# Instruction queues ordered by latest possible time instead of by age, in a planned long-convolution and FFN training step

## The chip, the cores and the metric

The kernel runs on one core of a Trainium2 chip. The metric is the device time in microseconds of one execution. Beside it stands one profiled execution, whose span is the time from its first to its last instruction.

## The reference

The kernel computes the output of a gated block and the gradients of all its inputs, for a sequence of 2048 rows of 512 channels in bf16. Cut to what matters:

```python
xn = layernorm(A_u)                                    # 2048 x 512
dt = exp(log_dt)                                       # per channel
P  = exp(dt * (A_re + 1j * A_im) * l)                  # 512 channels x 128 states x 2048 steps
K  = real(einsum("dn,dnl,dn->dl", C, P, dt * B))       # a long convolution kernel per channel
s  = irfft(rfft(xn) * rfft(K))[:2048] + xn * Dskip     # long convolution over the sequence
h  = silu(xn @ w1)                                     # 512 -> 1792
g  = silu(h @ w2)                                      # 1792 -> 512
out = A_u + s * g
# and the vector-Jacobian product with grad_out: gradients of A_u, A, B, C (re, im), log_dt, Dskip, w1, w2
```

## The kernel before

**Work and stages.** The channels are four blocks of 128. In order of the program: a setup (layer norm of the rows, constants, magnitudes of the state powers); the tables (`gen_tables`: sines on ACT, products on DVE, and on PE the convolution kernels' values), the forward convolutions by a discrete Fourier transform on PE (`gen_conv_x`, `gen_conv_fwd`), and beside them the FFN forward (`gen_ffn_fwd`, 8 chunks of 256 rows, L812 and L829); a gate stage (`gen_gate_rows`) that makes `ds` with Silu (L864) and `do` with its derivative (L873); the convolution backward (`gen_conv_bwd`) beside the FFN's backward for the activations (`gen_ffn_da`, L1173 and L1184, which loads `dhT` at L1149 and stores it at L1178); the state-space backward (`gen_ssm_bwd`, 16 groups of products, L961 to L1037) beside the rest of that; then the weight gradients (`gen_dw2` L1216, `gen_dw1` L1234) and the layer norm's backward (`gen_ln_bwd`, L1266 to L1279). Spectra, activations and tables that don't fit in SBUF go through DRAM. All evacuations of PSUM are in one helper, L295 on ACT and L296 on DVE.

**What sets the order.** The stages are Python generators, and `interleave`, `woven` and `paced` draw from them with fixed weights; that gives one order of all instructions, the program order. At its end `Plan` takes that list and makes a queue for each engine. It works out the dependencies (`deps`: reads, writes, buffers that are used again), and pairs that only say that one instruction may not start before another has started (`starts`: the first users of one tag's tiles in order, and pools that share memory). `cost` gives each instruction a time on its engine and a time to completion. `solve` then plays the program forwards in time: an instruction is ready when all it depends on is done, and when an engine is free it takes a ready instruction. Among those ready it takes the one with the smallest number, which is the oldest in program order: its age decides. DMAs are sent by the queue of the engine that issues them (SP for most), in the plan's order, and share one modelled line: 900 ns, the time of the packets, then 1200 ns to completion. A function on ACT whose table isn't loaded costs 1283 ns more. PE runs at half rate when a window of 3413 ns was too idle. `apply` fixes the result, by an order edge from each instruction to the next on its engine:

```python
        edge = mybir.DependencyInfo(mybir.DependencyClass.NoSync, mybir.DependencyReason.DATA)
        for line in self.plan.values():
            for a, b in zip(line, line[1:]):
                self.tc.add_manual_dep(self.ins[b], self.ins[a].name, edge, reason="plan")
```

On the chip each engine goes through its queue in that order, and waits where what it needs isn't there yet.

**The opening of the state-space backward.** `gen_ssm_bwd` first loads all six parameter matrices transposed (`load_params`, L609), then folds the gradients of block 0 (`ssm_fold`: four loads of `GE` at L961, then products on PE from L977), and loads the turned tables `YT` (L999) and `Eb` (L992) of the first group. All these go through SP's queue.

Of the kernel before, what the change touches and what calls it, by code (L numbers as in the profile page):

```python
# [34 lines left out]
class Plan:  # L35
# [5 lines left out]
    def __init__(self, nc, tc):  # L41
        self.tc, self.ins, self.deps, self.starts = tc, [], [], []
        cells, users, first, tags, pools, before, old, placed = {}, {}, {}, {}, {}, {}, {}, []
        held = {"left": [], "right": []}
        bounds = {p.alloc_inst.name: (p, True) for p in tc.info.pools}
        bounds.update({p.release_inst.name: (p, False) for p in tc.info.pools if p.release_inst is not None})
        for x in nc.cur_bb.bb.instructions:
            if x.name in bounds:
                p, opens = bounds[x.name]
                if str(p.space) == "SB":  # L50
                    h = held[str(p.side)]
                    if opens:
                        lo = h[-1][1] if h else 0
                        hi = lo + sum(m.bufs * m.max_size_bytes for m in p.tag_meta.values()) // P
                        h.append((p.id, hi))
                        placed.append((p.id, lo, hi) if str(p.side) == "left" else (p.id, self.ROOM - hi, self.ROOM - lo))
                    else:
                        h[:] = [y for y in h if y[0] != p.id]
                continue
            ap_of = lambda args: [a.bass_ap for a in args if getattr(a, "bass_ap", None) is not None]  # L60
            outs, ins = ap_of(x.outs), ap_of(x.ins)
            if not outs:
                continue
            n, eng, dep = len(self.ins), x.engine.name, set()
            if type(x).__name__ == "InstMatmult" and not x.start_tensor_calc:
                ins = ins + outs
            self.ins.append(x)
            spots = []
            for ap, writes in [(a, False) for a in ins] + [(a, True) for a in outs]:
                t = ap.tensor  # L70
                tag = getattr(t, "tag", None)
                if tag is None:
                    if not writes:
                        continue
                elif t.name not in users:
                    same = tags.setdefault(tag, [])
                    bufs = t.tag_meta.bufs
                    before[t.name] = first[same[-1]] if same and str(t.space) != "DRAM" else None
                    if len(same) >= bufs and str(t.space) != "DRAM":
                        old[t.name] = users[same[-bufs]]  # L80
                    same.append(t.name)
                    first[t.name], users[t.name] = n, set()
                if tag is not None:
                    dep |= old.get(t.name, set())
                    if before[t.name] is not None and before[t.name] != n:
                        self.starts.append((before[t.name], n))
                    users[t.name].add(n)
                    pools.setdefault(int(tag.rsplit("_", 1)[1]), set()).add(n)
                q, idx, size = self.cells(ap)
                last, readers = cells.setdefault(t.name, (np.full(size, -1, np.int32), {}))  # L90
                spots.append((writes, q, idx, last, readers))
                for k in q:
                    for r in [last] + (list(readers.values()) if writes else []):
                        dep.update(np.unique(r[k, idx]).tolist())
            for writes, q, idx, last, readers in spots:
                for k in q:
                    if writes:
                        last[k, idx] = n
                        for r in readers.values():
                            r[k, idx] = -1  # L100
                    else:
                        readers.setdefault(eng, np.full(last.shape, -1, np.int32))[k, idx] = n
            self.deps.append(dep - {-1, n})
        for i, (a, a0, a1) in enumerate(placed):
            for b, b0, b1 in placed[i + 1:]:
                if a0 < b1 and b0 < a1 and a in pools and b in pools:
                    self.starts.append((pools[a], pools[b]))

    @staticmethod
    def cells(ap):  # L110
# [71 lines left out]
                break  # L182
        return r

    def solve(self):

        N = len(self.ins)
        succ, wait = [[] for _ in range(N)], [len(d) for d in self.deps]
# [4 lines left out]
        groups = []  # L193
        for a, b in self.starts:
# [3 lines left out]
            else:  # L198
# [2 lines left out]
                    begun[m].append(-len(groups))  # L201
                for m in b:
                    wait[m] += 1
        cost = [self.cost(x) for x in self.ins]
        eng = [x.engine.name for x in self.ins]
        dma = ["DMA" in type(x).__name__ or "Dma" in type(x).__name__ for x in self.ins]
        ready = {e: [] for e in set(eng)}
        free = dict.fromkeys(ready, 0.0)
        line, tables = 0.0, "nesd"
        heat, warm = {}, {0: False}  # L210
        self.plan = {e: [] for e in ready}
        events, self.start = [], [0.0] * N
        for n in range(N):
            if not wait[n]:
                events.append((0.0, 1, n))
# [2 lines left out]
        end = 0.0  # L218

        def met(m, t):  # L220
            wait[m] -= 1
            when[m] = max(when[m], t)
            if not wait[m]:
                heapq.heappush(events, (when[m], 1, m))

        def clock(t):
            w = int(t // 3413)
            for v in range(max(warm), w):
                warm[v + 1] = heat.get(v, 0.0) / 3413 > (0.35 if warm[v] else 0.5)
            return warm[w]  # L230
        while events:
            t, kind, n = heapq.heappop(events)
            if kind == 1:
                heapq.heappush(ready[eng[n]], n)
                e = eng[n]
            else:
                e = n
            while ready[e] and free[e] <= t:
                n = heapq.heappop(ready[e])
                d, l = cost[n]  # L240
                if e == "PE":
                    if not clock(t):
                        l += max(d, 25.0)
                        d *= 2
                    heat[int(t // 3413)] = heat.get(int(t // 3413), 0.0) + d
                elif e == "Activation" and not dma[n]:
                    f = self.SETS.get(getattr(self.ins[n], "func", None))
                    if f:
                        both = "".join(c for c in f if c in tables)
                        if not both:  # L250
                            d, l = d + 1283.0, l + 1283.0
                        tables = both or f[0]
                self.plan[e].append(n)
                self.start[n] = t
                free[e] = t + d
                heapq.heappush(events, (free[e], 2, e))
                if dma[n]:
                    line = max(line, t + (d if e == "Pool" else min(d, 330.0)) + 900.0) + l
                    done = line + 1200.0
                else:  # L260
                    done = t + l + self.SEM
                end = max(end, done)
                for m in succ[n]:
                    met(m, t + d if e == "PE" == eng[m] else done)
                for m in begun[n]:
                    if m >= 0:
                        met(m, t)
                    else:
                        g = groups[-m - 1]
                        g[0] -= 1  # L270
                        if not g[0]:
                            for y in g[1]:
                                met(y, t)
        assert sum(map(len, self.plan.values())) == N, "the plan is not complete"
        return end

    def apply(self):
# [1015 lines left out]
def kernel(ctx, tc, A_u, A_A_re, A_A_im, A_B_re, A_B_im, A_C_re, A_C_im, A_log_dt, A_Dskip, B_x, B_w1, B_w2, grad_out,  # L1293
# [140 lines left out]
    es_b.close()  # L1434
    interleave([gen_ln_bwd(k, pool("lw", side="right")), dw], [1, 1])
    plan = Plan(nc, tc)
    plan.solve()
    plan.apply()
# [1 line left out]
_INS = ['A_u', 'A_A_re', 'A_A_im', 'A_B_re', 'A_B_im', 'A_C_re', 'A_C_im', 'A_log_dt', 'A_Dskip', 'B_x', 'B_w1', 'B_w2', 'grad_out']  # L1440
# [26 lines left out]
```

## Time and profile before

| | us |
|---|---|
| median of 3 runs | 701.69 |
| lowest, highest | 695.24, 705.36 |
| the profiled execution | 696.09 |
| its span | 694.4 |
| PE, DVE, ACT busy | 573.5, 521.0, 470.8 |
| mean granted TensorE clock | 0.950 |

The profile's page names groups of instructions by line, engine, and output and input tiles. PE is TensorE's matmuls, PEld its weight loads, DVE VectorE, ACT ScalarE, POOL GpSimd, SP SyncE; a name such as SPq is the engine's sequencer, which issues DMAs. A digit in a row of slices is the busy share of a fortieth of the span in tenths; PEclk is the clock that PE was granted, in tenths. In a timeline a row has its start, its duration, the engine, the line, the operation, the tiles and a count, and in brackets how long the engine was idle before it and what released it.

### The profile page before, as it was taken

Reading aid. Unit: us, or ns where it says so; the run is one execution under the profiler, and the core shown is the slowest. Engines: PE = TensorE matmul, PEld = TensorE weight load, DVE = VectorE, ACT = ScalarE, POOL = GpSimd, SP = SyncE. Lnnn points to the kernel's source line nnn. Section 1 sums busy time; section 2 is a strip of 40 time slices with the busy share of each in tenths; the row PEclk is TensorE's granted clock in tenths of the full one; section 3 lists DMA queues with packets and bytes.
Section 4 is the critical chain, followed back from the end, with each engine's and each line's share of the span. In section 5 each row is a group of like instructions: output and inputs, shape, how many; then the busy total and the mean of one; then the engine's idle time right before and its main releaser. Section 6 shows DMA issues by size and latency. Waiting matters only on the chain.

```text
span 694.4 us, 15206 instructions
## 1 busy us (share of the span) xinstructions
PE 573.5 (83%) x6268; PEld 416.6 (60%) x6268; DVE 521.0 (75%) x917; ACT 470.8 (68%) x630; POOL 79.9 (12%) x163
## 2 busy tenths in 40 slices
PE   0599697878979785469998998928998879999988
PEld 0455564547657564256765756626966656865877
DVE  6959987979989585869797979415798533966971
ACT  6959765978887988997867775406648438744541
POOL 1274100010001000000000000000002020023211
PEclk9989998999999998779999999978999999999999
DMA  9864536584557487968886775594899996747994
GB/s 297 331 145 154 196 142 225 206 274 168 189 192 260 178 292 259 287 227 274 263 273 204 236 228 176 144 236 116 168 215 221 223 252 147 172 124 243 261 253 124
DMA packets 158773, 148.85 MB, mean 214 GB/s; under 512 B 79280, under 2 KB 136112, under 8 KB 155120
## 3 DMA queue, kind: packets, MB, share of 16 engines
q1 hardware_dynamic: 145664, 125.07, 63.0%
q0 software_dynamic: 6144, 17.83, 7.1%
q10 hardware_dynamic: 6896, 4.98, 2.3%
q8 instruction: 49, 0.80, 0.5%
q14 instruction: 20, 0.16, 0.1%
HBM read 65.14 MB, written 64.36 MB: 187 GB/s over the span
## 4 chain that ended last, share of the span: by engine, by line
PE 48%; ACT 20%; DVE 13%; DMA 9%; issue 4%; SPq 4%; ACTq 2%; DVEq 0%
PE ps_w L1234 6%; PE ps_o L829 6%; PE ps_dx L1184 5%; PE ps_w L1216 5%; PE ps_da L1173 4%; ACT dA L295 4%; PE ps_h L812 2%; ACT mag_all L635 2%; PE psS L1032 2%; PE ps_i L573 2%; ACT sn L684 2%; PE pt_t L362 2%; PE ps_v L1010 2%; PE ps_i L582 2%; PE psS L1036 2%
## 5 line engine op out<-in xcount | busy, mean ns | idle before, releaser
L295 ACT CAST dA<-ps_s 128x1024 bf16<-128x1024 f32 x96 | 94.0, 1032 | 14.5 <-PE ps_s L541 9.9
L829 PE MATMUL ps_o<-W,aT 128*128 128x512 bf16 x224 | 62.8, 417 | 11.9 <-ACT hT L295 11.6
L812 PE MATMUL ps_h<-XT,W 128*128 128x256 bf16 x448 | 60.3, 279 | 6.5 <-DVE XT L296 5.0
L1173 PE MATMUL ps_da<-doT,W 128*128 128x256 bf16 x448 | 60.9, 276 | 3.1 <-ACT doT L295 1.8
L1020 DVE TENSOR_TENSOR Tp<-Vb,Eb 128x1344 bf16<-128x1344 bf16 x64 | 52.6, 855 | 10.2 <-ACT Vb L295 7.8
L1175 DVE TENSOR_TENSOR dhT<-ps_da,dhT 128x512 bf16<-128x512 f32 x56 | 37.7, 686 | 28.7 <-PE ps_da L1173 28.5
L295 ACT CAST dB<-ps_i 128x1024 bf16<-128x1024 f32 x48 | 47.0, 1027 | 17.3 <-PE ps_i L573 14.2
L295 ACT CAST Vb<-ps_v 128x672 bf16<-128x672 f32 x64 | 44.0, 740 | 18.8 <-PE ps_v L1010 15.2
L1184 PE MATMUL ps_dx<-W,dhT 128*128 128x512 bf16 x224 | 55.5, 380 | 0.0
L1216 PE MATMUL ps_w<-YD,a_tok 128*128 128x512 bf16 x224 | 53.4, 379 | 0.5 <-ACT a_tok L1201 0.5
L812 PEld LDWEIGHTS <-W 128*128 128x128 bf16 x448 | 42.4, 100 | 18.4 <-issue 10.9
L295 ACT CAST o<-ps_w 128x256 bf16<-128x256 f32 (+1 forms) x42 | 18.7, 445 | 50.0 <-PE ps_w L1234 28.1
L1234 PE MATMUL ps_w<-dh_tok,xn 128*128 128x256 bf16 x448 | 49.4, 273 | 3.1 <-DMA dh_tok<-DHd 3.1
L1173 PEld LDWEIGHTS <-W 128*128 128x128 bf16 x448 | 41.3, 99 | 13.4 <-issue 6.2
L1234 PEld LDWEIGHTS <-xn 128*128 128x128 bf16 x448 | 43.7, 98 | 8.9 <-DMA dh_tok<-DHd 2.1
L829 PEld LDWEIGHTS <-aT 128*128 128x128 bf16 x224 | 21.2, 105 | 37.9 <-issue 17.9
L573 PE MATMUL ps_i<-I,sp_in 64*128 64x128 bf16 x768 | 32.5, 229 | 11.6 <-DVE sp_in L596 8.7
L573 PEld LDWEIGHTS <-sp_in 64*128 64x128 bf16 x768 | 23.8, 99 | 24.5 <-DVE sp_in L596 12.3
L295 ACT CAST hT<-ps_h 128x512 bf16<-128x512 f32 x56 | 32.1, 617 | 8.1 <-PE ps_h L812 4.9
L296 DVE COPY dB<-pt_f 128x2048 bf16<-128x2048 bf16 x24 | 28.3, 1218 | 11.4 <-PE pt_f L547 11.4
L557 PE MATMUL ps_s<-dB,F 128*64 128x512 bf16 x192 | 29.5, 389 | 7.1 <-ACT dA L295 5.3
L295 ACT CAST pd_s<-ps_dx 128x512 bf16<-128x512 f32 x16 | 9.4, 590 | 35.7 <-DMA Pd<-pd_s 17.0
(222 smaller groups left out, 1301.9 us busy)
## 6 DMA issues: line engine op xcount, KB each, us to landing
Yd<-YD SPq DMA_DIRECT2D x8, 1024.0 KB, 5.3
sp_in<-Ud SPq DMA_DIRECT2D x8, 1024.0 KB, 8.1
h_in<-Hd SPq DMA_DIRECT2D x14, 512.0 KB, 4.8
Ed<-E SPq DMA_DIRECT2D x8, 672.0 KB, 4.0
Eb<-Ed SPq DMA_DIRECT2D x8, 672.0 KB, 5.6
Hd<-hT POOLq DMA_DIRECT2D x8, 512.0 KB, 5.8
Ud<-dA SPq DMA_DIRECT2D x4, 1024.0 KB, 4.8
KXd<-dA SPq DMA_DIRECT2D x4, 1024.0 KB, 6.0
```

What stands on the lines that cost most here:

```text
L295: return self.nc.scalar.copy(out=out, in_=in_)
L296: return self.nc.vector.tensor_copy(out=out, in_=in_)
L557: nc.tensor.matmul(out=ps[64 * h:64 * h + 64, 4 * v:4 * v + 4], lhsT=k.F2[:, c, :], rhs=Bv[:, u, v, h], start=True, stop=True)
L573: nc.tensor.matmul(out=ps[:, h, g], lhsT=Y[hs, c, 4 * q + g, :], rhs=k.I2[hs, c].rearrange("p c m -> p (c m)"), start=(c == 0), stop=(c == 1))
L812: nc.tensor.matmul(out=ps[:, j], lhsT=k.W1[:, dk, ft * P:ft * P + P], rhs=XTv[:, :, dk, :], start=(dk == 0), stop=(dk == DK - 1))
L829: nc.tensor.matmul(out=ps[:], lhsT=aT[:, ft, t * P:t * P + P], rhs=k.W2[:, ft, :], start=(ft == 0), stop=(ft == FT - 1))
L1020: k.nc.vector.tensor_tensor(out=Tp[:, c, :, r ^ c].rearrange("p e (q w) a -> p q w e a", w=2), in0=Vb[:, :, c].rearrange("p q w (e a) -> p ...
L1173: nc.tensor.matmul(out=ps[:, j], lhsT=k.W2[:, ft, dk * P:dk * P + P], rhs=dTv[:, :, dk, :], start=(dk == 0), stop=(dk == DK - 1))
L1175: nc.vector.tensor_tensor(out=dh[:, i0:i0 + 2, :], in0=ps[:], in1=dh[:, i0:i0 + 2, :], op=ALU.mult)
L1184: nc.tensor.matmul(out=ps[:], lhsT=dhs[ft // 8][:, ft % 8, t * P:t * P + P], rhs=k.W1[:, :, ft * P:ft * P + P], start=(ft == 0), stop=(ft ...
L1216: nc.tensor.matmul(out=ps[:], lhsT=at[:, t, :], rhs=k.do[:, t, :], start=(t == 0), stop=(t == k.T - 1))
L1234: nc.tensor.matmul(out=ps[:], lhsT=k.xn[:, t, dk * P:dk * P + P], rhs=dh[:, t].rearrange("p j n -> p (j n)"), start=(t == 0), stop=(t == k ...
```

## The change

`solve` takes a list `age` by which the ready instructions are ranked. A new function `back` plays the same program from its end backwards, with the same costs: an instruction is ready when all that depend on it are placed, and among those ready on an engine the one that the forward plan completed last goes first. It returns for each instruction how long before the end it must start at the latest. `search` runs `solve` once by age, then six times `back` and `solve` in turn, where the instruction with the longest time to the end goes first; the plan with the shortest modelled end of these six is kept (the plan by age isn't one of them). New pairs in `starts` make the last user of each tile, in program order, start after all its other users. No instruction of the device is added or taken away. `back` knows no function tables and no slow PE clock; `solve` still does. The diff, cut:

```diff
             self.deps.append(dep - {-1, n})
+        self.starts += [(m, max(u)) for u in users.values() for m in u if m != max(u)]
...
-    def solve(self):
+    def solve(self, age):
...
             if kind == 1:
-                heapq.heappush(ready[eng[n]], n)
+                heapq.heappush(ready[eng[n]], (age[n], n))
                 e = eng[n]
             else:
                 e = n
             while ready[e] and free[e] <= t:
-                n = heapq.heappop(ready[e])
+                n = heapq.heappop(ready[e])[1]
...
-                end = max(end, done)
+                end, self.done[n] = max(end, done), done
...
+    def back(self):
+
+        N, cost, eng, dma = len(self.ins), self.costs, self.eng, self.dma
+        left, before, groups = [0] * N, [[] for _ in range(N)], []
+        for d in self.deps:
+            for m in d:
+                left[m] += 1
...
+        need, late = [0.0] * N, [0.0] * N
+        ready = {e: [] for e in set(eng)}
+        free = dict.fromkeys(ready, 0.0)
+        line, queue, events = 0.0, [], []
+
+        def met(m, t):
+            left[m] -= 1
+            need[m] = max(need[m], t)
+            if not left[m]:
+                heapq.heappush(events, (need[m], 2, m) if dma[m] else (max(0.0, need[m] - cost[m][0]), 1, m))
+        for n in range(N):
+            if not left[n]:
+                left[n] = 1
+                met(n, 1200.0 if dma[n] else cost[n][1])
+        while events:
+            t, kind, n = heapq.heappop(events)
+            if kind == 2:
+                heapq.heappush(queue, (-self.done[n], n))
+            if kind > 1 and kind < 4:
+                while queue and line <= t:
+                    n = heapq.heappop(queue)[1]
+                    line = t + cost[n][1]
+                    heapq.heappush(events, (line, 3, n))
+                    d = cost[n][0]
+                    heapq.heappush(events, (line + 900.0 - (0.0 if eng[n] == "Pool" else max(0.0, d - 330.0)), 1, n))
+                continue
+            if kind == 1:
+                heapq.heappush(ready[eng[n]], (-self.done[n], n))
+                e = eng[n]
+            else:
+                e = n
+            while ready[e] and free[e] <= t:
+                n = heapq.heappop(ready[e])[1]
+                free[e] = late[n] = t + cost[n][0]
+                heapq.heappush(events, (free[e], 4, e))
+                for m in self.deps[n]:
+                    met(m, late[n] + (1200.0 if dma[m] else cost[m][0] if e == "PE" == eng[m] else cost[m][1] + self.SEM))
...
+        return late
+
+    def search(self, rounds):
+
+        self.solve(range(len(self.ins)))
+        best = None
+        for _ in range(rounds):
+            end = self.solve([-t for t in self.back()])
+            if best is None or end < best[0]:
+                best = end, self.plan, self.start
+        end, self.plan, self.start = best
+        return end
...
-    plan.solve()
+    plan.search(6)
     plan.apply()
```

More of the change, by code (lines that the diff above doesn't have):

```diff
@@ L107, in __init__ @@
                     self.starts.append((pools[a], pools[b]))
+        self.costs = [self.cost(x) for x in self.ins]
+        self.eng = [x.engine.name for x in self.ins]
+        self.dma = ["DMA" in type(x).__name__ or "Dma" in type(x).__name__ for x in self.ins]
     @staticmethod
@@ L203, in solve @@
                     wait[m] += 1
-        cost = [self.cost(x) for x in self.ins]
-        eng = [x.engine.name for x in self.ins]
-        dma = ["DMA" in type(x).__name__ or "Dma" in type(x).__name__ for x in self.ins]
+        cost, eng, dma = self.costs, self.eng, self.dma
         ready = {e: [] for e in set(eng)}
@@ L211, in solve @@
         self.plan = {e: [] for e in ready}
-        events, self.start = [], [0.0] * N
+        events, self.start, self.done = [], [0.0] * N, [0.0] * N
         for n in range(N):
@@ L274, in solve @@
         assert sum(map(len, self.plan.values())) == N, "the plan is not complete"
+        return end
[5 more added lines that the diff above has]
+                left[m] += 1
+        for a, b in self.starts:
+            if isinstance(a, int):
+                before[b].append(a)
+                left[a] += 1
+            else:
+                groups.append([len(b), a])
+                for m in b:
+                    before[m].append(-len(groups))
+                for m in a:
+                    left[m] += 1
+        need, late = [0.0] * N, [0.0] * N
[26 more added lines that the diff above has]
+                e = eng[n]
+            else:
+                e = n
[5 more added lines that the diff above has]
+                    met(m, late[n] + (1200.0 if dma[m] else cost[m][0] if e == "PE" == eng[m] else cost[m][1] + self.SEM))
+                for m in before[n]:
+                    if m >= 0:
+                        met(m, late[n])
+                    else:
+                        g = groups[-m - 1]
+                        g[0] -= 1
+                        if not g[0]:
+                            for y in g[1]:
+                                met(y, late[n])
+        return late
```

## The prediction

> **What bounds the kernel now.** I first read the top of the page: busy times, then the slices.
>
> ```profile
> span 694.4 us, 15206 instructions
> PE 573.5 (83%) x6268; PEld 416.6 (60%) x6268; DVE 521.0 (75%) x917; ACT 470.8 (68%) x630; POOL 79.9 (12%) x163
> PE   0599697878979785469998998928998879999988
> PEclk9989998999999998779999999978999999999999
> ```
>
> No engine is full. PE has the most work, 573.5 of 694.4 us, so 121 us of it are gaps, and the slices show where: the first two, four around slice 15, one hole at slice 26 (a 2), and a tenth to a third of every slice between 4 and 14. I cut the span there, into five stages, and asked for the busy times of each.
>
> ```profile
> 35.00:260.00 225.00, 190.12 (x2123) 131.04 (x2123) 192.71 (x277) 175.77 (x249) 34.13 (x43) 0.95 0.58 201
> 260.00:315.00 55.00, 32.43 (x375) 25.50 (x374) 37.41 (x54) 51.48 (x51) 0.56 (x1) 0.78 0.82 262
> 315.00:441.00 126.00, 120.91 (x1478) 82.49 (x1478) 108.08 (x152) 88.51 (x100) 6.48 (x12) 0.99 0.71 227
> 441.00:471.00 30.00, 15.37 (x113) 10.48 (x111) 7.34 (x13) 6.04 (x6) 0.00 (x0) 0.84 0.84 211
> 471.00:694.00 223.00, 204.53 (x2109) 158.88 (x2106) 145.75 (x341) 120.16 (x185) 31.25 (x56) 0.97 0.83 194
> ```
>
> The columns are stretch, length, busy PE, weight load, DVE, ACT, POOL, granted clock, DMA share, GB/s. PE's gaps: 34.9 us in the tables and the forward passes (DVE is the fuller engine there, with 32.3 us left), 22.6 in the gate stage (ACT has 3.5 left), 5.1 in the convolution backward, 14.6 where the state-space backward opens, 18.5 to the end. The last stage is PE's: what starts it earlier should end the kernel earlier. The chain that ended last agrees that this is a matter of order rather than of one engine:
>
> ```profile
> PE 48%; ACT 20%; DVE 13%; DMA 9%; issue 4%; SPq 4%; ACTq 2%; DVEq 0%
> ```
>
> The change adds no device work. Every matmul, cast and transfer is the same; each engine's queue is in another order, so its cost is the sum of stalls gained and lost.
>
> **The opening of the state-space backward, 441 to 471.** Its timeline is where age as a rule visibly costs.
>
> ```profile
> 441.65 1.69 SPq L609 DMA_TRANSPOSE par_Ar<-in_A_A_re_dram  x1
> ...
> 448.60 1.26 SPq L609 DMA_TRANSPOSE par_Ci<-in_A_C_im_dram  x1
> ...
> 449.91 0.70 SPq L961 DMA_DIRECT2D GE<-dKd  x1
> ...
> 459.95 0.77 SPq L1178 DMA_DIRECT2D DHd<-dhT  x1
> ...
> 466.61 0.38 SPq L1149 DMA_DIRECT2D dhT<-Hd  x1
> ...
> 467.04 0.59 SPq L961 DMA_DIRECT2D GE<-dKd  x1
> ...
> 470.46 0.58 PE L977 MATMUL G<-GE,zero 128*128 128x512 bf16 x1 [14.07 <-DMA dhT<-Hd]
> ```
>
> Six parameter transposes, older because the generator emits them first, stand ahead of the first GE load. The fold on PE (L977) waits for the fourth GE load, at 467.04; that one stands behind a dhT load, which waited for the DHd store issued at 459.95. PE stands 14.07 us. The parameters serve the gradients of block 0, which need four groups of products first, whereas GE heads the whole chain. By latest time GE and YT go ahead of the transposes. The GE loads can move by 449.91 − 441.65 = 8.3 us. I take **−8.3**. At most the gap goes, −14.1; at worst the order only trades one late load for another, and a second stall of the same size appears, +14.1.
>
> At this place the Trainium skill has a rule, in "TensorE: Matmul & The Clock Gate", Part 1: PE's clock halves after an idle window of some 3.4 us. The trace's granted clock of 0.84 in this stretch agrees. By the rule half of one cold window, an estimated 1.7 us, would go with the stall; the sum here is −8.3, by the rule −10.
>
> **Tables and forward, 35 to 260.** Three views: PE's waits in this stage, then DVE's and SP's.
>
> ```profile
> PE ps_o L829 <- ACT hT L295: 11.6, 5, 4.1
> PE ps_h L812 <- DVE XT L296: 4.6, 1, 4.6
> DVE E L692 <- ACT sn L684: 14.4, 6, 4.8
> SPq L694 <- DVE E L692: 92.5, 8, 22.2
> ```
>
> (Total us, times, longest.) FFN products and table work share ACT: PE waits for hT casts and DVE for sines, each up to about 4 us, whichever was younger. A backward plan can put the side with the longer remainder first; it can't make the 192.7 us of DVE work shorter. All it can win is DVE's slack of 32.3 us; a loss I bound by the PE wait doubling, +11.6. I take a quarter of the slack, **−8.1**: half the 14.4 + 4.6 us of waits for sines and XT is 9.5, the row it is nearest to. The SP row is idle time in the queue's order, not work: loads behind a table store that isn't ready wait with it, under either rule, so I put nothing for it.
>
> **The gate stage, 260 to 315.** ACT is the bound, and part of its time is function tables.
>
> ```profile
> L873 ACT ACT_TABLE_LOAD x3 | 3.8, 1283 | 0.1
> L864 ACT ACT_TABLE_LOAD x2 | 2.6, 1283 | 0.0
> ```
>
> L864 is the Silu that makes ds, L873 the derivative that makes do. ds feeds the long convolution backward and do its filler, so by latest time the L864s go together: two loads instead of five is 3 × 1.283 = **−3.8**. The forward plan charges a switch but doesn't avoid one; no saving and as many more is +3.8, and at best −6.4 go.
>
> **The start.**
>
> ```profile
> 5.21 0.69 DVE L512 BATCH_NORM_STATS2 st<-x_sb 128x6 f32<-128x512 bf16 x1 [5.21 <-DMA x_sb<-in_A_u_dram]
> ...
> 17.49 0.18 DVE L515 TENSOR_SCALAR ve<-mv 128x4 f32<-128x4 f32 x1
> ...
> 20.05 1.89 PE L362 MATMUL pt_t<-ident,xn 128*128 128x128 bf16 x16 [20.05 <-DVE xn L522]
> ```
>
> Four statistics at 0.69 and four aggregates at 0.18 are 3.5 us, yet they end at 17.5, as older DVE work on twiddles and indices goes between. Done at once, PE would start about 8 us earlier, at 12. But the next 225 us are DVE's rather than PE's, so I credit a quarter, **−2**; bounds −8 and, if the magnitudes are delayed by the same 3.5 us, +3.5.
>
> **What it costs: transfers.** Both directions of the plan use the same formulas: 900 ns to the queue's turn, the packets, 1200 ns to completion. For a 1024 KB sp_in (128 packets of 8 KB at 364 ns over 16 engines, 330 ns to issue) they give 5.3 us, for a dhT load of 1024 packets of 512 B at 28 ns 4.2 us.
>
> ```profile
> sp_in<-Ud SPq DMA_DIRECT2D x8, 1024.0 KB, 8.1
> dhT<-Hd SPq DMA_DIRECT2D x8, 512.0 KB, 5.0
> PE ps_w L1234 <- DMA dh_tok<-DHd: 3.1, 2, 1.8
> PE ps_v L1010 <- DMA YT<-Yd: 3.0, 1, 3.0
> ```
>
> Measured: 8.1 and 5.0. So latest times of loads come out 0.8 to 2.8 us too late, and where age sent a load early for no reason, the new order may send it when it is already due. PE's direct waits for loads are small (3.1 and 3.0 here). I let these grow by two thirds: **+4**. From below nothing; above, all eight sp_in<-Ud loads late by 2.8 is +22.
>
> The Trainium skill speaks for the planner here: "DMA: Bandwidth & Descriptors", Anatomy of one DMA, has about 2.0 us fixed plus the bytes at 436 GB/s. By it a 512 KB load takes an estimated 3.2 us, less than the plan allows; the trace's 5.0 us disagrees. By the rule this term would be 0 and the sum 4 us lower.
>
> **The new edges**, by which the last user of a tile in program order starts after its other users, cost nothing here. The one that could hold the end is xn, whose last user is the last L1234 product.
>
> ```profile
> 676.83 1.41 DVE L1277 SCALAR_TENSOR_TENSOR o<-xn,m,Gt 128x512 bf16<-128x512 bf16 x2 [1.59 <-DMA out_dram<-o]
> 677.13 14.13 PE L1234 MATMUL ps_w<-dh_tok,xn 128*128 128x256 bf16 x128 [1.32 <-DMA dh_tok<-DHd]
> ```
>
> The last other user starts at 676.83 and PE works to 691: 14 us of cover. Were it gone, that final row group's 1.41 us would be added.
>
> **Sum:** −8.3 − 8.1 − 3.8 − 2 + 4 = −18.2 us. The profiled execution took 696.09 us, 1.7 over its span; that gives 677.9. The median of the runs, 701.69, is 5.6 above the profiled one, so the forecast is **683.5 us**, 2.6% below the median. Before's runs span 695.24 to 705.36, so about 2% (14 us) is what a measurement can tell from no change.
>
> **The rivals.**
> *The gain stays in the plan* (within 2%, chance 0.35). The stall at 441 shrinks, but the last stage has its DMA engines 0.83 busy and the YT and dh_tok transposes queue there, so the 8.3 us return as later waits; in the forward stage DVE is already 86% busy and wins a small part. −8.3 + 8.3 − 3.8 − 2 + 4 is about −2, or 700. For it: DVE, PE and ACT are all above 75% in the forward stage. Against: PE does have 18.5 us of gaps in the last stage to absorb shifts.
> *Stalls by the SP queue* (slower by over 2%, chance 0.19). SP is in order: a load waiting for a buffer holds everything behind it, as dhT held GE at 466.61. With young, "urgent" loads put ahead, each stage joint (forward to gates, gates to backward, backward to state space) can have such a stall of 14.1 us; three of them with none of the gains, +4, is 46 at the worst; two with the gains of tables and start lost, 2 × 14.1 − 8.3 − 3.8 + 4 = +20, 722 us. It decides from two new stalls of over 10 us. For it: loads are planned too short. Against: the greedy pass still sends a load as soon as it is ready when SP is free, under both rules.
> *It doesn't do what it says* (inside the 0.35). The plan by age isn't among the six, and the shortest is by modelled time; if the six are no shorter on the chip, the orders differ and the time is 695 to 705.
> *More than the forecast* (chance 0.12, counted as faster). Half of DVE's slack, −16.2, and all of the 14.1: −8.1 and −5.8 more, 669.6 us.
>
> Faster by over 2%: 0.34 for the forecast and 0.12 for more, 0.46; within 2%, 0.35; slower, 0.19. The unknown terms are independent enough that I don't add all bounds: the range goes from 8 us under the stronger gain, 662, to 709, which has the whole of the second case and stops short of the two-stall case. Faster cases alone: 662 to 688.
>
> **What would show it.** In the changed kernel's timeline, GE's four loads ahead of the par transposes, and the PE wait at L977 down from 14.07 to about 6; three or fewer table loads at L864 and L873; the first PE instruction near 12 to 16; waits of PE for sp_in, YT and dh_tok not above some 12 us in total. I am wrong if a new hole of over 10 us stands at a stage joint, if DVE's busy share between 35 and 260 stays at 86%, or if the gaps of PE after the state-space backward opens grow from 18.5 by what the stall gave back.

## The result, and the profile after

| | before | after |
|---|---|---|
| median, us | 702.37 (4 runs) | 677.35 (4 runs) |
| lowest to highest | 695.24 to 705.36 | 675.85 to 684.58 |
| profiled execution, span | 696.09, 694.4 | 675.85, 673.8 |

The changed kernel is faster: the ratio is 0.968, 95% interval 0.958 to 0.978, some 22.5 us. Below, line numbers of the changed kernel are 78 higher than before's for the same code. Its page, for the rows that were shown of before:

```profile
span 673.8 us, 15178 instructions
PE 573.3 (85%) x6236; PEld 419.8 (62%) x6268; DVE 521.5 (77%) x917; ACT 466.0 (69%) x628; POOL 89.3 (13%) x163
...
PE   0659868999797998679999999959979899899978
...
PE 38%; DMA 12%; ACT 8%; DVE 8%; SPq 4%; issue 2%; ACTq 0%; DVEq 0%
```

The work is the same to the microsecond on PE and DVE; ACT has 4.8 us less, of which 2.6 are two function table loads. (The 32 matmuls that PE seems to have lost are records missing from the trace: the weight loads are 6268 in both. The chain of after could be followed back over 72% of the span only, so its shares can't be held against before's.) What went is idle time. In the slices, the four around slice 15 and the hole at slice 26 are shallower. The five stages, with the cuts moved to where the stages now end:

```profile
35.00:239.00 204.00, 172.10 (x1917) 121.88 (x1932) 185.60 (x263) 162.68 (x233) 34.08 (x39) 0.95 0.62 218
239.00:298.00 59.00, 45.91 (x554) 35.83 (x557) 40.24 (x57) 54.97 (x60) 2.85 (x4) 0.88 0.79 255
298.00:424.00 126.00, 121.11 (x1484) 81.91 (x1483) 111.22 (x156) 95.06 (x103) 6.50 (x12) 1.00 0.74 236
424.00:451.00 27.00, 19.06 (x132) 12.91 (x131) 8.64 (x15) 6.95 (x7) 0.00 (x0) 0.87 1.00 234
451.00:673.00 222.00, 201.82 (x2077) 157.67 (x2090) 144.68 (x339) 119.62 (x184) 31.24 (x56) 0.98 0.85 195
```

The forward stage is 21 us shorter (204 for 225), the gate stage 4 longer, the opening 3 shorter, the rest as it was. PE's gaps (length less busy) say where the idle time was taken: forward 34.9 to 31.9, gate stage 22.6 to 13.1, opening 14.6 to 7.9, the end 18.5 to 20.2. So PE's idle time went mostly from the gate stage and the opening, while the forward stage got shorter because 18 us of PE's work left it (190.1 to 172.1). The first instructions of a line and the last give the milestones; in such a row stand the count, the shortest, median and longest in ns, and the starts of the first and the last. Before, then after: the second of the tables' steps on DVE, and the last products of the tables on PE.

```profile
L682 DVE TENSOR_SCALAR V<-V x16: 1151/1217/1516, 55.5 to 227.0; 128x2048 int32<-128x2048 int32 x8, 128x1920 int32<-128x1920 int32 x8
L729 PE MATMUL ps_e<-Xr,SEL x96: 219/246/379, 96.8 to 257.2; 128*128 128x224 bf16 x32, 128*128 128x128 bf16 x32, 128*128 128x512 bf16 x16, 128*128 128x160 bf16 x16
```
```profile
L760 DVE TENSOR_SCALAR V<-V x16: 1145/1214/2532, 43.5 to 209.9; 128x2048 int32<-128x2048 int32 x8, 128x1920 int32<-128x1920 int32 x8
L807 PE MATMUL ps_e<-Xr,SEL x94: 219/259/634, 92.6 to 236.7; 128*128 128x224 bf16 x32, 128*128 128x128 bf16 x32, 128*128 128x160 bf16 x16, 128*128 128x512 bf16 x14
```

The tables start 12 us earlier and end 20.5 us earlier, and 20.6 us is what the span lost. So by the end of the forward the whole lead is there. That doesn't mean that the later stages add nothing: they do 15 us more of PE's work than before (387.9 for 373.2) in the same time, and for that their gaps had to be filled. One of these is the opening of the state-space backward, where the prediction put its largest single term.

### The profile page after: what moved, and what is told of

Its sections match the earlier page's. It is cut to its first block, busy times and chain, and to the rows that moved or that the text cites. A ratio compares the mean times of both kernels' runs of the same rounds, so it can differ in the third digit from the quotient of the medians.

```text
span 673.8 us, 15178 instructions
## 1 busy us (share of the span) xinstructions
PE 573.3 (85%) x6236; PEld 419.8 (62%) x6268; DVE 521.5 (77%) x917; ACT 466.0 (69%) x628; POOL 89.3 (13%) x163
## 4 chain that ended last, share of the span: by engine, by line
PE 38%; DMA 12%; ACT 8%; DVE 8%; SPq 4%; issue 2%; ACTq 0%; DVEq 0%
PE ps_dx L1262 6%; PE ps_w L1294 5%; PE ps_da L1251 4%; DMA YT<-Yd 4%; PE ps_w L1312 3%; PE ps_i L660 2%; PE pt_t L440 2%; PE psS L1114 2%; PE psS L1110 2%; PE ps_v L1088 2%; PE ps_i L651 2%; PE ps_s L635 2%; ACT dA L373 2%; DMA Kd<-KE 2%; DMA dhT<-Hd 2%
## 5 line engine op out<-in xcount | busy, mean ns | idle before, releaser
L890 PE MATMUL ps_h<-XT,W 128*128 128x256 bf16 x448 | 66.8, 299 | 4.9 <-ACT hT L373 2.8
L890 PEld LDWEIGHTS <-W 128*128 128x128 bf16 x448 | 45.9, 107 | 17.4 <-issue 7.5
L907 PE MATMUL ps_o<-W,aT 128*128 128x512 bf16 x209 | 52.4, 381 | 4.0 <-ACT aT L898 2.4
L1251 PEld LDWEIGHTS <-W 128*128 128x128 bf16 x448 | 41.2, 99 | 14.4 <-issue 6.6
L907 PEld LDWEIGHTS <-aT 128*128 128x128 bf16 x224 | 20.2, 98 | 26.2 <-issue 3.7
L1228 ACT ACTIVATE dhT<-dhT 128x2048 bf16<-128x2048 bf16 (+1 forms) x16 | 26.9, 1706 | 11.1 <-DMA dhT<-Hd 10.1
L619 PEld LDWEIGHTS <-TF 128*128 128x128 bf16 x384 | 25.6, 102 | 14.5 <-issue 4.5
```

The source lines that it names most:

```text
L890: nc.tensor.matmul(out=ps[:, j], lhsT=k.W1[:, dk, ft * P:ft * P + P], rhs=XTv[:, :, dk, :], start=(dk == 0), stop=(dk == DK - 1))
L907: nc.tensor.matmul(out=ps[:], lhsT=aT[:, ft, t * P:t * P + P], rhs=k.W2[:, ft, :], start=(ft == 0), stop=(ft == FT - 1))
L1228: nc.scalar.activation(out=dh[:, 0:n], in_=dh[:, 0:n], func=ACT.Derivative_silu)
L1251: nc.tensor.matmul(out=ps[:, j], lhsT=k.W2[:, ft, dk * P:dk * P + P], rhs=dTv[:, :, dk, :], start=(dk == 0), stop=(dk == DK - 1))
```

## The experiments

Two theories were on trial. **S**: the setup makes the gain (its rows are normalised earlier, so the tables may start earlier), with the forward behind it. **P**: the prediction's own sum, 8 us at the opening, 8 in the forward, 2 at the start. Each ratio is to before, run on the same chip on the same occasion; 1% is 7 us. The medians come from several occasions, on which before took 697.9 to 702.4 us, so across rows the ratios are compared.

| run | ratio | 95% interval | median us |
|---|---|---|---|
| edges alone, order by age | 1.007 | 1.004 to 1.010 | 704.14 |
| latest times in the setup only | 0.988 | 0.984 to 0.993 | 689.98 |
| latest times everywhere but the setup | 0.980 | 0.974 to 0.987 | 684.37 |
| latest times from the state-space backward on | 0.999 | 0.996 to 1.002 | 697.53 |
| latest times up to the state-space backward | 0.979 | 0.972 to 0.987 | 683.46 |
| before, `ones` by memset | 1.001 | 0.997 to 1.005 | 699.08 |
| before, layer norm emitted first | 1.005 | 1.001 to 1.008 | 700.02 |
| before, parameters behind the first group | 1.001 | 0.998 to 1.004 | 698.68 |
| before, GE loads planned as independent | 0.985 | 0.980 to 0.990 | 688.56 |
| before, both of layer norm and GE | 0.988 | 0.984 to 0.993 | 690.35 |
| after, the worst of its six plans | 0.988 | 0.983 to 0.994 | 689.73 |
| after, GE loads planned as independent | 0.958 | 0.952 to 0.963 | 668.27 |

**The edges.**

```diff
-    plan.search(6)
+    plan.solve(range(len(plan.ins)))
```

> The order by age of before, with nothing of the change but the new edges (last user of a tile starts after its other users). The prediction put them at 0, with 14 us of cover at the one place it looked at: 700 to 703. Rival: edges on tiles other than xn bind somewhere in the middle, and some us are lost, 704 to 710.

The rival was right: 0.7% slower, about 5 us. By the traces the first transform of `ds` comes 3.7 us later (307.9 for 304.2), and at the end PE's last products wait longer for their transposed loads, 3.1 us before and now:

```profile
PE ps_w L1312 <- DMA dh_tok<-DHd: 7.6, 3, 4.6
```

So the two halves of the change that follow, which both have the edges, are to be read against 704 as well as 700.

**Latest times in one half.** The instructions up to the tables' memory form the setup; `cut` is its end. Each run has one of the two last lines; the names behind them are the runs'.

```diff
-            end = self.solve([-t for t in self.back()])
+            late = self.back()
+            end = self.solve([-1e9 - t if n < cut else n for n, t in enumerate(late)])    # setup_late
+            end = self.solve([n - 1e9 if n < cut else -t for n, t in enumerate(late)])    # setup_age
```

> Latest times rank only the setup's instructions (all before the tables); everything younger is ranked by age, as before, with the change's new edges. Theory S (the two traces' milestones: the tables' first V starts at 43.5 instead of 49 to 55 us, last normalised rows end at 30 instead of 42, and most of the gap to the end is there by then): V starts near 38 to 44 and the time falls by 8 to 14 us against before, to about 690. Theory P (the prediction's own sum: start worth 2 us, the opening of the state-space backward 8, the forward 8): within 4 us of before, about 700.

> The opposite half: the setup is ranked by age and goes first, everything younger by latest time. Theory S: the tables start about 12 us later than in the changed kernel and the end moves by 8 to 14 us, to 686 to 691. Theory P: 2 us are lost, 679 to 680.

The setup alone is worth 8 us against before and 13 against the edges alone: within S's 8 to 14. The other half seems worth more, 14 and 18.5, though the two intervals overlap a little (from 0.984, to 0.987), and its time lies between what the two theories gave for it. S was right that the start matters, and it isn't shown that it carries most; P was wrong on both. One caution holds for every run with latest times: each keeps another plan of six, and two plans of one rule differ by 12 us below, so differences of a few us between these runs can be the plan rather than the part that was taken away. The trace of the second half shows how the forward gains. The stretch from the tables' last products to the first transform of ds, in before, in the changed kernel and in setup_age:

```profile
257.00:304.00 47.00, 27.56 (x325) 21.10 (x323) 32.82 (x49) 43.39 (x51) 0.56 (x1) 0.75 0.89 283
```
```profile
237.00:286.00 49.00, 40.30 (x473) 29.75 (x475) 31.68 (x44) 45.85 (x59) 2.85 (x4) 0.90 0.75 242
```
```profile
244.00:291.00 47.00, 35.72 (x459) 26.68 (x459) 31.90 (x45) 43.32 (x54) 2.29 (x3) 0.89 0.74 246
```

PE works 40.3 and 35.7 us there, where it worked 27.6; with latest times in the setup only it is 29.8:

```profile
248.00:295.00 47.00, 29.82 (x327) 22.68 (x327) 32.20 (x48) 42.22 (x49) 0.56 (x1) 0.72 0.88 274
```

FFN products were moved out of the forward, where they had stood ahead of the longer chain of tables and convolutions, into the stage in which PE had been waiting: of PE's work in these stretches 4.8 us are the FFN's forward products (L812 and L829) in before and 17.2 in the changed kernel. The chain's fullest engine in the forward shows the other side (70 to 210 us, before and after; DVE is the third pair):

```profile
70.00:210.00 140.00, 113.83 (x1304) 79.04 (x1303) 125.50 (x178) 106.95 (x158) 11.98 (x13) 0.95 0.56 199
```
```profile
70.00:210.00 140.00, 119.06 (x1404) 87.69 (x1412) 135.32 (x189) 113.43 (x165) 12.04 (x14) 0.95 0.61 219
```

DVE went from 90% to 97% busy in this stretch.

**Single causes in the setup, by hand.** Two edits of before, order by age.

```diff
-    G.affine_select(out=ones[:], in_=k.xn[:, 15, 0:128], compare_op=ALU.is_equal, fill=1.0, base=1,
-                    pattern=[[0, 128]], channel_multiplier=0)
+    G.memset(ones[:], 1.0)                                  # before_ones
...
-        next(consts)
         ln = layer_norm(k, wp, x_sb)
         next(ln)
         k.XT = [turned_rows(k, k.fp, k.xn, c, "XT", k.evx) for c in range(2)]
-        next(ln)
+        run(ln)                                             # before_ln
+        next(consts)
         next(consts)
-        next(ln)
         ssm_weights(k, wp, S)
-        next(ln)
         run(consts)
```

> Before, with one thing changed: the tile ones is filled by a memset, so that POOL's chain of selects no longer waits for the last normalised rows (L459). Nothing of the order rule is changed. If theory S has the right mechanism (the tables' memory is the setup's, so they may start only when the last select has started; the selects wait for xn of the last rows), V starts at about 40 instead of 49 us and the time falls by 6 to 10 us, to about 694. If the tables' start doesn't carry to the end (the forward is bound by DVE's work alone, theory P's view of the start), V moves and the time stays within 3 us of before.

> Before, order by age, with the layer norm of all 16 row tiles emitted ahead of the constants and the state-space weights, so that it is older. It does by hand what latest times were seen to do in the setup. If the late end of the layer norm is what held the setup (theory S), the last normalised rows end near 31 instead of 42 us, the second V starts near 44 and the time falls by 8 to 13 us, to 687 to 692. If something else in the setup's new order mattered, or the gain needs an order by latest time behind it, within 4 us of before.

Neither gains. In the first, POOL's reciprocal roots came later, and with them the last normalised rows (at 46.9 instead of 41.8 us), so the tables' V started only 5 us sooner by the same line. The second does what it was made for and still fails:

```profile
L522 DVE TENSOR_SCALAR xn<-x_sb,rstd,nb x16: 394/404/655, 16.1 to 34.3; 128x512 bf16<-128x512 bf16 x16
L682 DVE TENSOR_SCALAR V<-V x16: 1147/1210/2601, 46.3 to 228.7; 128x2048 int32<-128x2048 int32 x8, 128x1920 int32<-128x1920 int32 x8
L729 PE MATMUL ps_e<-Xr,SEL x93: 218/233/380, 90.5 to 256.8; 128*128 128x224 bf16 x32, 128*128 128x128 bf16 x32, 128*128 128x160 bf16 x16, 128*128 128x512 bf16 x13
```

V starts 9 us sooner, and the last products come at 256.8, where they came at 257.2. The forward by age gave the head start back. With the setup by latest time (and the new edges) it did not, though the forward goes by age there too:

```profile
L814 PE MATMUL ps_e<-Xr,SEL x95: 219/233/379, 86.8 to 247.9; 128*128 128x224 bf16 x32, 128*128 128x128 bf16 x32, 128*128 128x160 bf16 x16, 128*128 128x512 bf16 x15
```

So S's mechanism, the late end of the layer norm, is not shown. The setup's new order as a whole is worth 8 us; which part of it keeps the gain through the forward stays open.

**The opening.** One edit does by hand what the prediction costed, the other takes away what the planner believes of the GE loads. `cells` marks a tile by quarters of 32 partitions; a GE load writes every fourth partition, so each of the four seemed to write over the one before, and was planned after it had landed.

```diff
-    par = load_params(k, sb, 0, k.D)
-    par["dt"] = k.dt[:]
...
             vb[i] = ssm_v(k, q0, half[i // 2][0], yt.pop(i), sb)
+            if par is None:
+                par = load_params(k, sb, 0, k.D)            # before_par
+                par["dt"] = k.dt[:]
...
-            q, dims, g, room = range(p0 // 32, p1 // 32 + 1), ap.ap[1:], 64 // size, (4, pitch * size // 64 + 1)
+            q = (p0 % 4,) if s // pitch == 4 else range(p0 // 32, p1 // 32 + 1)         # before_ge, after_ge
+            dims, g, room = ap.ap[1:], 64 // size, (4, pitch * size // 64 + 1)
```

> Before, with the six parameter transposes of the state-space backward emitted after the first group's products, so that by age they no longer stand ahead of the first GE load. It does by hand the one reordering to which the prediction gave 8.3 us. Theory P: the first GE load comes 8 us sooner after the last dUd store, the wait of PE at the fold falls from 14 to about 6 us, and the time falls by 6 to 8 us. Rival G (four GE loads that the planner takes to depend on one another, each planned after the one before has landed, set the fold's start whatever stands ahead of the first): the first GE load moves, the fold moves by 0 to 3 us, and the time stays within 3 us of before.

> Before, order by age, with one line of the planner's dependencies changed: a tile written with a partition step of 4 counts as four separate quarters, so that the four GE loads (and the KE stores' reads) are no longer planned one behind the other. Rival G: the four GE loads go out together, the first fold's wait of PE falls from 14 us to under 6, and as three more folds follow, the time falls by 8 to 15 us, to 685 to 692. Theory P: the parameter transposes still stand ahead of GE, so at most the three gaps between the GE loads go, some 5 us.

Timeline of the first, the parameters moved:

```profile
442.14 0.70 SPq L961 DMA_DIRECT2D GE<-dKd  x1
...
448.35 0.61 SPq L961 DMA_DIRECT2D GE<-dKd  x1
...
458.77 0.59 SPq L961 DMA_DIRECT2D GE<-dKd  x1
...
463.60 0.61 SPq L961 DMA_DIRECT2D GE<-dKd  x1
...
469.23 0.61 PE L977 MATMUL G<-GE,zero 128*128 128x512 bf16 x1 [13.88 <-DMA GE<-dKd]
```

The first GE load went 7.8 us sooner, much as the prediction had it, but the fourth only 3.4 (463.60 for 467.04) and the fold 1.2; PE's wait is 13.88 for 14.07, and the time is the same. Now the loads as independent, with the parameters still ahead of them:

```profile
453.62 2.66 SPq L962 DMA_DIRECT2D GE<-dKd  x4
...
458.63 0.38 PE L978 MATMUL G<-GE,zero 128*128 128x512 bf16 x1 [2.00 <-DMA GE<-dKd]
```

All four in 2.7 us, the wait 2.0, and 1.5% faster. G was right and P wrong: what holds the fourth load is that three others stand ahead of it in the plan, each to land first, and not the transposes, which here still go ahead of all four. (The line holds for all four folds, so the 10 us are not this one's alone.) The changed kernel has the same chain, 22 us long:

```profile
424.74 0.69 SPq L1039 DMA_DIRECT2D GE<-dKd  x1
425.49 1.68 SPq L687 DMA_TRANSPOSE par_Ar<-in_A_A_re_dram  x1
...
445.56 1.01 PE L440 MATMUL pt_t<-ident,YD 128*128 128x128 bf16 x8 [5.85 <-DVE dhT L1253]
...
446.71 0.59 SPq L1039 DMA_DIRECT2D GE<-dKd  x1
...
450.74 0.39 PE L1055 MATMUL G<-GE,zero 128*128 128x512 bf16 x1 [1.18 <-DMA GE<-dKd]
```

PE waits only 1.18 us here because other products stand ahead of the fold, not because GE is there sooner: from the last `dUd` store to the fold it is 26.7 us, and was 29.3. A part of the gap has moved ahead, to the wait of 5.85.

> The changed kernel with the same line changed. If the opening is still limited by the chain of GE loads (22 us from the first to the fourth in its trace, against 17 before), the fold comes some 12 us sooner and the time falls by 6 to 14 us, to 663 to 671. If PE has enough other work there (7 us of gaps in the stretch 441 to 471), it falls by 0 to 5 us.

Its timeline, and the same stretch of 27 us in which the change has PE at 19.06:

```profile
430.28 3.77 SPq L1040 DMA_DIRECT2D GE<-dKd  x4
...
437.26 0.38 PE L1056 MATMUL G<-GE,zero 128*128 128x512 bf16 x1 [0.40 <-DMA GE<-dKd]
```
```profile
424.00:451.00 27.00, 25.72 (x241) 18.72 (x240) 16.67 (x20) 14.03 (x17) 0.54 (x1) 1.00 0.96 239
```

With the loads independent the fold starts 7 us after the first GE load instead of 26, and the granted clock is 1.00 where the change has 0.87 and before had 0.84. The Trainium skill's rule ("TensorE: Matmul & The Clock Gate", Part 1: an idle window halves the clock) agrees with these three: the clock is full only where the gap is gone. The median of 668.27 is the lowest of all kernels here. Its interval, 0.952 to 0.963, overlaps that of the change, 0.958 to 0.978, and the two were timed on separate occasions, so that it beats the change by about 1% is likely rather than shown.

> Both edits by hand on the order by age: the layer norm emitted first, and the GE loads planned as independent. If the two terms add, 8 to 13 and 10 us, the time is 675 to 682, that of the changed kernel, without any latest times. If they overlap, 684 to 690.

The two hand edits don't add: 0.988 is no better than GE alone. The change is not just these two things.

**The rest of the change, from the state-space backward on.**

```diff
+            end = self.solve([n if n < cut else 1e9 - t for n, t in enumerate(late)])     # ssm_late
+            end = self.solve([-1e9 - t if n < cut else n for n, t in enumerate(late)])    # ssm_age
```

> Latest times rank only what comes from the state-space backward's first parameter load on; everything older is ranked by age and goes first; with the new edges. It keeps the opening's share of the change and drops the setup's and the forward's. Theory S: no more than 3 to 4 us below the kernel with the edges alone (704 us), so about 700. Theory P: 8 to 9 us below it, about 695.

> Latest times rank everything older than the state-space backward's first parameter load; from there on age decides. Theory S: the setup and the forward carry nearly all of the change, so 677 to 683. Theory P: 8 us of the gain are lost, 684 to 688.

The first is 0.8% (some 6 us) below the edges alone, between the two theories. The second loses 8 us against the change (0.979 for 0.968, with intervals that overlap), nearer to P's figure. Both put latest times from there on at 6 to 8 us. The traces show two places. One is the opening: in ssm_age, whose trace is like the changed kernel's up to there (the tables end at 236.8, for 236.7), PE stands 12.5 us ahead of the first fold (the view gives "issue": no releaser is seen). In the 27 us that end with this fold PE works 11.4 to 12.4 us in the four kernels of one GE chain that go by age from there on (before, edges alone, setup_late, ssm_age), and 18.7 to 22.1 in the four that go by latest times (ssm_late, setup_age, the worst plan and the changed kernel). The other is the very end, in the waits for dh_tok: 6.7 us in ssm_age, 3.4 in the changed kernel. (The last row is before's wait for YT over the whole span.)

```profile
PE G L1062 <- issue: 12.5, 1, 12.5
PE ps_w L1319 <- DMA dh_tok<-DHd: 6.7, 2, 4.1
```
```profile
PE ps_w L1312 <- DMA dh_tok<-DHd: 3.4, 1, 3.4
PE ps_v L1088 <- DMA YT<-Yd: 5.0, 6, 2.0
```
```profile
PE ps_v L1010 <- DMA YT<-Yd: 3.3, 2, 3.0
```

**The choice among six.**

```diff
-            if best is None or end < best[0]:
+            if best is None or end > best[0]:
```

> The changed kernel, but of its six plans the one with the longest modelled end is kept. If the choice among the six is worth what the plans' ends say, it is slower than the changed kernel by some 5 to 10 us, 683 to 688. If the rule by latest time carries the gain and the six plans are alike on the chip, within 4 us of 677.

It costs 12 us against the change by the medians, 14 by the ratios, more than half of the gain. Same rule, same costs, same edges. The loss is spread over the kernel. The last products of the tables and the first transforms of ds in the worst plan, then the transforms in the kept one:

```profile
L807 PE MATMUL ps_e<-Xr,SEL x94: 218/259/631, 92.0 to 241.3; 128*128 128x224 bf16 x32, 128*128 128x128 bf16 x32, 128*128 128x160 bf16 x16, 128*128 128x512 bf16 x14
...
L619 PE MATMUL ps_s<-ds,TF x128: 216/219/315, 296.8 to 381.7; 128*128 128x128 bf16 x128
```
```profile
L619 PE MATMUL ps_s<-ds,TF x128: 219/219/314, 286.4 to 372.0; 128*128 128x128 bf16 x128
```

The tables end 4.6 us later (241.3 for 236.7) and `ds` is there 10.4 us later (296.8 for 286.4), 5.8 us more. The span is 15.0 us longer (688.8 for 673.8), so another 4.6 come after that.

## Why the prediction was right, point by point

The time lay in the range, 6 us below the forecast of 683.5, between it and the stronger case (669.6): on the side that was given the most, 0.46 for faster by over 2%. The profiled executions differ by 20.2 us, for a sum of 18.2. The mechanism, idle time taken out by order alone, was right. Most of the terms were not.

- **The opening, −8.3.** This step failed. The prediction named the fourth GE load rightly as that which the fold waits for, but took it to be late because of the transposes ahead of the first, so that all four would move by 8.3 us. The four are planned one behind the other: moving the transposes brought 0 (1.001), making the loads independent 10 us. In the changed kernel only the first load goes ahead of the transposes, the fourth behind all six. What it does gain at this place, a gap of PE of 7.9 us for 14.6, it gains by other work in front of the fold; that these 6.7 us come near 8.3 is luck.
- **Forward, −8.1.** Right in kind, too small: latest times outside the setup are worth 18.5 us against the edges alone, 6 to 8 of them from the state-space backward on, so some 10 to 12 here, by subtraction: no run had latest times in the forward alone. The prediction would have been wrong had DVE's share between 35 and 260 stayed at 86%. Taken by the letter it nearly did, 195.1 of 225 us, 87%; but the stage now ends at 239, and over the stage it is 91% (185.6 of 204). The stage's 21 us are 13.9 of DVE's slack (32.3 to 18.4, some of it the earlier start of the tables) and 7.1 of DVE's work that left the stage with the filler. This second part the prediction had ruled out, by bounding the term by the slack of one stage.
- **Gates, −3.8.** The loads of function tables fell from five to three, where the sum had two, so 2.6 us for 3.8, by the rows

```profile
L951 ACT ACT_TABLE_LOAD x2 | 2.6, 1283 | 0.0
...
L942 ACT ACT_TABLE_LOAD x1 | 1.3, 1283 | 0.0
```

  but the stretch did not get shorter (47 us before, 49 after). With the FFN's last products moved into it, the stage is full of other work.
- **The start, −2.** The first PE instruction came at 15.64, in the forecast's 12 to 16. The term was mis-sized: 8 us, 13 against the edges alone, outside the bound of −8 by the latter. The prediction had argued that PE's start isn't binding; the tables' start moved by 12 us.
- **Transfers, +4.** Right in direction, half the size: waits of PE for dh_tok and YT rose from 6.4 to 8.4. The 3.2 us that would have made this term 0 have no support here: the 512 KB loads of dhT took 5.0 us before and 5.9 after.
- **Edges, 0.** Failed: +5 us with the order by age. The argument looked at one tile, xn, and at the cover of its last user. What they cost with latest times no run shows.
- The terms as measured against one another (−13 setup, −11 forward, −7 from the opening on, +5 edges) come to −26 for −22.5 measured: they overlap, or the plans' differences enter. That the sum of the prediction came out near is luck in part.
- The rival that the queue of SP would bring new stalls didn't happen: the change has no PE wait over 10 us behind the start. The rival that the plan's gain isn't the chip's was the more serious one: the worst of the six plans keeps less than half of it.

## What to carry to other kernels

Here the order by the time to the end let filler leave the stage in which the long chain runs and fill a later hole; look for PE's gap in one stage and PE's filler in another before bounding the gain by one stage's slack. Look at what the planner believes about a stall before blaming the order: here four loads were planned one behind the other for a conflict that wasn't there, and one line of dependencies was worth 10 us to the old rule. Two plans of the same rule differed by 12 us on the chip; so a single plan's gain of a few us says little of the rule. In the one pair tried, the plan with the longer modelled end was also the slower one on the chip, which speaks for making several and keeping the best.

## What the runs showed of the hardware that was not expected

With the loads planned as independent (the run before_ge), the four strided GE loads of 128 KB each were issued in 2.66 us, and the fold began 2.35 us after the last issue had ended. In the orders of before and of the change, where each was planned behind the one before, their issues stood 4 to 9 us apart.
